# Attention in pairs of chunks: fp32 projections on quarters of the TensorE array, sums and numerators on halves

## The chip, the cores and the metric

The kernel runs on one core of a Trainium2 chip. The metric is the device time of one execution in microseconds. Three runs of the kernel before gave 926.39 us as their median (924.83 to 926.86).

## What is computed

A linear attention with random features (4 batches, 8 heads, 576 tokens, head size 64, 128 features), whose output of 2304 x 512 goes through two feed-forward blocks. All of it is in float32.

```python
def phi(x):
    proj = np.einsum('bhsd,md->bhsm', x, omega)
    sq = np.sum(x * x, axis=-1, keepdims=True) / 2.0
    h = proj - sq
    h = h - np.max(h, axis=-1, keepdims=True)
    return np.exp(h) / np.sqrt(m)
q_p, k_p = (phi(q_s), phi(k_s))
kv = np.einsum('bhsm,bhsd->bhmd', k_p, v)
z = np.sum(k_p, axis=2)
num = np.einsum('bhsm,bhmd->bhsd', q_p, kv)
den = np.einsum('bhsm,bhm->bhs', q_p, z)[..., None] + 1e-06
...
x = (x @ w_in) * sigmoid(x @ w_in) @ w_out
g = x @ w_gate
out = (g * sigmoid(g) * (x @ w_val)) @ w_out2
```

The term `sq` is the same for all features of a token, so it drops out against the row's maximum; the kernel leaves it out in both versions.

## The kernel before

**Stages.** The attention runs first (about the first 146 us), then the first feed-forward block (its upward products at L1066, its downward products at L1433), then the second one (the same lines). In the feed-forward blocks each fp32 product is made of three fp32r products of split operands, in seven products of Strassen's kind. The change touches the attention and the few instructions in which it hands over to the first upward phase.

**The attention's tiling.** The 32 pairs of batch and head are taken as 8 units `u`. A unit holds two heads (`h`) side by side on the 128 partitions of q and k, and two batches one after the other (`b`), so it has 1152 tokens, which are 9 chunks of 128 tokens. The fifth chunk of a unit holds the end of one batch and the beginning of the next one (64 tokens each). `step(s)` works on chunk s of 72; nothing is reordered, every engine runs its instructions in the order in which `step` writes them.

**One step.** `proj(s + 1)` makes the projections of q and k of the next chunk: six fp32r matmuls of 256 columns, three for each of q and k (high part times high part, low times high, high times low), where the 256 columns are the features of both heads, with zeros off the diagonal of omega. `soft(s)` takes the maxima of the four groups of 128 features on DVE (one reduction, `nb`) and then four exponentials on ACT (`kq`). `kv_tr(s - 2)` adds k' times v (and k' times ones) into a PSUM bank, two fp32 matmuls of 65 columns (four in the straddling chunk), and turns q' with two transposes; every second chunk ACT copies the turned q' of two chunks from PSUM to SBUF (`qp`, L816). When a batch has ended, DVE copies its sums out (`st`, L826) and the numerators follow two or more steps later: `num(u, g)` for three chunks (fp32 matmuls of 65 columns, 12 records in a plain group of three chunks, since an fp32 matmul is two records), `divide` on DVE, `turn` (three transposes), `take_out` on DVE, and one `store` for a unit.

**Splits.** q and k arrive as three pieces of 384 tokens per unit. `split_piece` makes the high and the low part of each piece on POOL (L706 and L708), for the first two pieces of the first unit partly on DVE.

**Banks.** PSUM has 8 banks. Projections and turned q' take banks 0 to 4 in rotation (`rot`), sums and numerators share banks 5 to 7 (`px`).

**Filling.** While the attention runs, `feed` puts in work for the stage after it, at most one instruction per engine and step for the stream "conv" (weights that are converted from 64-bit words and split: L343 and L408 on ACT, L350, L357, L406 and L419 on DVE, L376 on POOL) and a few for the stream "x" (the first block's input: L571 on ACT, L580 on DVE, L601). A consumer of an ACT or DVE result may go in one step later than its producer.

**Hand-over.** After the last step the last numerators of the last unit (two groups) are made inside the upward phase (`last_nums`, `last_turn`): `mark` writes a bank once (L1043) as soon as its divide has read it, so that the products can take it.

Of the kernel before, what the change touches and what calls it, by code (L numbers as in the profile page):

```python
# [9 lines left out]
F32 = mybir.dt.float32  # L10
# [32 lines left out]
def kernel(  # L43
# [21 lines left out]
    UB = 2  # L65
# [600 lines left out]
    rot = [0, 1, 2, 3, 4]  # L666
    px = deque((5, 6, 7))

    def bank():
        rot.append(rot.pop(0))  # L670
        return ps[rot[-1]].rearrange("p (a b) -> p a b", a=2)
# [10 lines left out]
    raw, hl, kq, qp, kvps = {}, {}, {}, {}, {}  # L682
# [14 lines left out]
    def load_piece(u, nm, i):  # L697
        raw[u, nm, i] = t = ap1.tile([P, CW], F32, tag=f"raw{nm}", name=f"raw{nm}", bufs=3)
        nc.sync.dma_start(out=t, in_=(kT if nm == "k" else qT)[u, :, i * CW : (i + 1) * CW])
# [15 lines left out]
    om = cut(fa, SUM_AT, 2 * M)  # L715
    zero = const.tile([P, M], F32, name="zero")
    nc.vector.memset(zero, 0.0)
    load_piece(0, "k", 0)
    for h in range(2):
        nc.sync.dma_start(out=om[h * D : (h + 1) * D, h * M : (h + 1) * M], in_=omT)  # L720
    load_piece(0, "q", 0)
    load_v(0, nc.scalar)
    for h in range(2):
        nc.vector.memset(om[h * D : (h + 1) * D, (1 - h) * M : (2 - h) * M], 0.0)
# [6 lines left out]
    for i in range(1, 3):  # L731
        for nm in ("k", "q"):
            load_piece(0, nm, i)
# [9 lines left out]
    PIECES = {3: (1, 0), 4: (1, 1), 6: (1, 2), 7: (1, 3), 0: (0, 4), 1: (0, 5)}  # L743
    pieces = [(nm, i) for i in range(3) for nm in ("k", "q")]


    act_q, dve_q, pps = [], [], {}
# [12 lines left out]
    def soft(s):  # L760
        ps = pps.pop(s)


        nb = ap1.tile([P, 4], F32, tag="nb", name="nb", bufs=3)
        nc.vector.reduce_max(nb, ps.rearrange("p i (h m) -> p (i h) m", h=2), axis=AX.X, negate=True)  # L765
        e = ap1.tile([P, 2, 2 * M], F32, tag="kq", name="kq", bufs=4)
        for i in range(2):
            for h in range(2):
                nc.scalar.activation(  # L769
                    e[:, i, h * M : (h + 1) * M],  # L770
                    ps[:, i, h * M : (h + 1) * M],
                    AF.Exp,
                    bias=nb[:, 2 * i + h : 2 * i + h + 1],
                )
        kq[s] = e
# [866 lines left out]
```

## Time and profile before

| | |
|---|---|
| runs, median | 926.39 us (924.83 to 926.86) |
| profiled execution, its own time | 926.11 us |
| span in the profile | 924.3 us |
| first product of the first upward phase (L1066) | 146.09 us after the span's start |
| PE busy, whole span | 905.0 us (98%) |
| DVE, ACT, POOL busy, whole span | 657.7, 558.4, 197.0 us |

The span is the time from the first to the last instruction; the execution's own time is 1.8 us longer. Busy time of PE counts matmuls in flight, which overlap, so that a busy PE is not PE at its peak. In the trace an fp32 matmul stands as two records, an fp32r matmul and a transpose as one.

### The profile page before, as it was taken

What the parts mean: (1) busy time and instruction counts of PE and PEld (TensorE: products, weight loads), DVE (VectorE), ACT (ScalarE), POOL (GpSimd) and SP (SyncE); (2) the same over time, 40 slices, a digit from 0 to 9 for tenths busy, and PEclk for the clock granted to TensorE, in tenths of its full rate; (3) what the DMA queues carried; (4) which work ended last, traced back from release to release, by engine and by line L of the source; (5) the groups of instructions that cost most, each with busy time, mean ns of one, the idle gap of its engine ahead of it and who ended that gap; (6) DMA issues with size and microseconds to landing.
All of it is one profiled execution on the core that took longest, in us unless ns stands there. A gap on an engine that the chain in (4) does not pass through costs nothing.

```text
span 924.3 us, 15768 instructions
## 1 busy us (share of the span) xinstructions
PE 905.0 (98%) x5591; PEld 895.3 (97%) x5591; DVE 657.7 (71%) x1055; ACT 558.4 (60%) x1190; POOL 197.0 (21%) x244
## 2 busy tenths in 40 slices
PE   8999999999999998999999999999999999999998
PEld 8999999999999998999999899999999999899998
DVE  4898986857574398586689899574747447968584
ACT  5788785876667675455457765554455447445453
POOL 6676951104343100000000014221303010000000
PEclk9999999999999999999999999999999999999999
DMA  7576515848989991715613755562626159371701
GB/s 218 183 235 208 174 50 197 271 157 275 317 291 358 349 382 58 232 55 163 206 43 109 244 164 187 174 201 79 213 68 222 47 184 314 114 240 52 237 16 69
DMA packets 109888, 169.94 MB, mean 184 GB/s; under 512 B 9200, under 2 KB 93808, under 8 KB 109808
## 3 DMA queue, kind: packets, MB, share of 16 engines
q1 hardware_dynamic: 108640, 168.33, 55.8%
q8 instruction: 44, 0.72, 0.3%
q10 hardware_dynamic: 1168, 0.59, 0.2%
q14 instruction: 36, 0.29, 0.1%
HBM read 107.02 MB, written 61.87 MB: 183 GB/s over the span
## 4 chain that ended last, share of the span: by engine, by line
PE 90%; DVE 4%; DMA 3%; ACT 2%; issue 1%; SPq 0%; DVEq 0%; ACTq 0%
PE ps L1066 43%; PE ps L1433 31%; PE ps L843 3%; PE ps L789 3%; PE ps L755 2%; PE ps L756 2%; PE ps L757 2%; PE ps L805 2%; DMA g_d<-fa 1%; PE ps L868 1%; DVE ra L1296 1%; DMA fa<-in_moe_w_in 1%; DVE ra L419 0%; DMA ra<-wu_val 0%; DVE fa L1124 0%
## 5 line engine op out<-in xcount | busy, mean ns | idle before, releaser
L376 POOL TENSOR_TENSOR fa<-fa 128x256 f32<-128x256 f32 x136 | 112.6, 841 | 529.0 <-DVE fa L357 301.3
L1066 PE MATMUL ps<-ra 128*128 128x384 f32 x840 | 156.3, 335 | 3.0 <-ACT ps L1083 3.0
L1066 PE MATMUL ps<-rb,ra 128*128 128x384 f32 x840 | 157.3, 340 | 0.0
L1066 PE MATMUL ps<-rc,ra 128*128 128x384 f32 x840 | 156.8, 339 | 0.0
L1066 PEld LDWEIGHTS ps<-ra 128*128 128x128 f32 x840 | 146.7, 188 | 4.3 <-ACT ps L1083 4.3
L1066 PEld LDWEIGHTS ps<-rb,ra 128*128 128x128 f32 x840 | 148.7, 188 | 0.3 <-ACT ps L1083 0.3
L1066 PEld LDWEIGHTS ps<-rc,ra 128*128 128x128 f32 x840 | 148.6, 188 | 0.1
L1083 ACT ACTIVATE ps<-ps 128x384 f32<-128x384 f32 x180 | 85.5, 476 | 88.7 <-PE ps L1066 82.1
L1140 DVE TENSOR_TENSOR fa<-fa,ps 128x384 f32<-128x384 f32 x120 | 66.2, 552 | 100.5 <-ACT ps L1083 78.1
L1292 ACT ACTIVATE ra<-fa 128x768 fp32r<-128x768 f32 x105 | 88.0, 844 | 81.2 <-PE ps L1433 64.4
L1296 DVE TENSOR_TENSOR ra<-fa,ra 128x768 fp32r<-128x768 f32 x105 | 100.5, 957 | 50.5 <-PE ps L1433 31.9
L1433 PE MATMUL ps<-ra,rb 128*128 128x384 f32 x720 | 129.4, 340 | 0.0
L1433 PEld LDWEIGHTS ps<-ra,rb 128*128 128x128 f32 x720 | 127.8, 189 | 0.8 <-DVE ra L1296 0.6
L1433 PE MATMUL ps<-ra 128*128 128x384 f32 x612 | 109.7, 337 | 6.7 <-DVE ra L1296 6.5
L1433 PEld LDWEIGHTS ps<-ra 128*128 128x128 f32 x612 | 106.7, 189 | 8.8 <-DVE ra L1296 8.0
L769 ACT ACTIVATE kq<-ps,nb 128x128 f32<-128x128 f32 x288 | 83.1, 403 | 25.3 <-DVE nb L765 24.1
L1433 PE MATMUL ps<-ra,rc 128*128 128x384 f32 x432 | 78.2, 340 | 1.6 <-DVE ra L1296 1.6
L1433 PEld LDWEIGHTS ps<-ra,rc 128*128 128x128 f32 x432 | 76.1, 188 | 2.7 <-DVE ra L1296 2.7
L1107 ACT ACTIVATE fa<-fa 128x384 f32<-128x384 f32 x84 | 43.8, 522 | 28.8 <-DVE fa L1140 28.5
L1316 DVE TENSOR_TENSOR fa<-ra,fa 128x768 f32<-128x768 f32 x63 | 60.1, 954 | 0.7
L1292 ACT ACTIVATE ra<-ra 128x768 fp32r<-128x768 f32 x42 | 35.5, 845 | 36.0 <-PE ps L1433 32.1
L1296 DVE TENSOR_TENSOR ra<-ra 128x768 fp32r<-128x768 f32 x42 | 40.2, 958 | 20.9 <-PE ps L1433 9.3
(100 smaller groups left out, 1227.6 us busy)
## 6 DMA issues: line engine op xcount, KB each, us to landing
g_d<-fa SPq DMA_DIRECT2D x168, 192.0 KB, 3.4
fa<-g_d SPq DMA_DIRECT2D x42, 384.0 KB, 4.4
ra<-g_d SPq DMA_DIRECT2D x42, 384.0 KB, 4.1
fa<-in_moe_w_out SPq DMA_DIRECT2D x28, 512.0 KB, 5.3
fa<-in_moe_w_in SPq DMA_DIRECT2D x16, 512.0 KB, 5.0
wd_out<-fa SPq DMA_DIRECT2D x14, 512.0 KB, 3.3
fa<-in_moe_w_gate SPq DMA_DIRECT2D x12, 512.0 KB, 3.9
fa<-in_moe_w_val SPq DMA_DIRECT2D x12, 512.0 KB, 5.2
```

The costliest lines, as they stand in the source:

```text
L376: f(blk(f"S{n}"), blk(l), blk(r))
L769: nc.scalar.activation(e[:, i, h * M : (h + 1) * M], ps[:, i, h * M : (h + 1) * M], AF.Exp, bias=nb[:, 2 * i + h : 2 * i + h + 1],)
L789: nc.tensor.matmul(acc[:, o : o + VH], e[a:z, 0, h * M : (h + 1) * M], v_t[u % 2][a:z, c, o : o + VH], start=first and h == 0, stop=last, ...
L843: nc.tensor.matmul(acc[a:z, o : o + VH], qp[u][:, h, c * P + a : c * P + z], st[u, b][:, h * VH : (h + 1) * VH], start=True, stop=True, sk ...
L1066: nc.tensor.matmul(ps[b][:, :N], cut(l, j * P, P), cut(r, j * N, N), start=start and c == 0, stop=stop and c == 5, skip_group_check=True,)
L1083: nc.scalar.activation(out() if callable(out) else out, src, AF.Copy)
L1107: nc.scalar.activation(b["t"], src, AF.Silu)
L1140: nc.vector.tensor_add(t, t if in_place else p5[n], ps[bank_][:, :N])
L1292: nc.scalar.activation(ops[s, p, k][0], src(), AF.Copy)
L1296: nc.vector.tensor_sub(l, src(), h.bitcast(F32))
L1316: (nc.gpsimd if eng == "POOL" else nc.vector).tensor_sub(z(PLACE[to]), z(PLACE.get(l, l)), z(PLACE.get(r, r)))
L1433: nc.tensor.matmul(ps[BANKS[p] + e][:, :N], cut(a, e * P, P), b, start=p in FIRST and i == 0 and c == 0, stop=p in LAST and i == fp - 1 an ...
```

## The change

`two_steps(d)` takes the place of `step(s)` and works on a pair of chunks; 36 pairs make the attention.

- `proj(d)` uses fp32 matmuls on q and k as they arrived. Each has 64 rows of the array (one head) and 64 columns of it (half a chunk's tokens), so that four of them stand on the four quarters of the array; omega has 128 columns for each. A pair of chunks takes 16 of them. The two heads write into different banks; a pair takes two banks, and pairs alternate between banks 0, 1 and 2, 3.
- The splits of q and k (`split_piece`) and of omega are gone, and so is POOL's share of this stage but for `feed`. q and k of a unit arrive as one transfer each, except for the first unit.
- `soft(d)` has one reduction and four exponentials for each bank, as many of both as before. Divides stand between the two reductions.
- `kv` and `num` are written as halves: each matmul yields 64 of the 128 output partitions.
- `q_turn(d)` turns q' of both chunks into bank 4, and one copy on ACT takes the 512 columns out.
- `feed` is called twice for a pair, at its end. Three groups of numerators are left for the upward phase where there were two.

```diff
-    rot = [0, 1, 2, 3, 4]
     px = deque((5, 6, 7))
...
-    def split_piece(u, nm, i):
-        hi, lo = hl[u, nm, i] = tuple(
-            ap1.tile([P, CW], F32R, tag=f"{x}{nm}", name=f"{x}{nm}", bufs=3) for x in ("hi", "lo")
-        )
-        t = raw.pop((u, nm, i))
-        nc.gpsimd.tensor_scalar(hi, t, 1.0, 1.0, op0=ALU.mult, op1=ALU.mult)
-        eng = nc.vector if u == 0 and i < 2 else nc.gpsimd
-        eng.tensor_sub(lo, t, hi.bitcast(F32))
-        if u + 1 < NU and u > 0:
-            load_piece(u + 1, nm, i)
+    def load_raw(u, nm, i=None):
+        if not i:
+            raw[u, nm] = ap1.tile([P, UT], F32, tag=f"raw{nm}", name=f"raw{nm}", bufs=2)
+        src = kT if nm == "k" else qT
+        a, z = (0, UT) if i is None else (i * CW, (i + 1) * CW)
+        nc.sync.dma_start(out=raw[u, nm][:, a:z], in_=src[u, :, a:z])
...
-    om_hi = const.tile([P, 2 * M], F32R, name="om_hi")
-    om_lo = const.tile([P, 2 * M], F32R, name="om_lo")
-    nc.vector.tensor_scalar_mul(om_hi, om, SCALE)
-    nc.vector.scalar_tensor_tensor(om_lo, om, SCALE, om_hi.bitcast(F32), op0=ALU.mult, op1=ALU.subtract)
...
+    nc.vector.tensor_scalar_mul(om, om, SCALE)
...
-    def proj(s):
-        u, c = divmod(s, NCH)
-        ps = bank()
-        for i, nm in enumerate(("k", "q")):
-            hi, lo = hl[u, nm, c // 3]
-            cs = slice((c % 3) * P, (c % 3 + 1) * P)
-            nc.tensor.matmul(ps[:, i, :], hi[:, cs], om_hi, start=True, stop=False)
-            nc.tensor.matmul(ps[:, i, :], lo[:, cs], om_hi, start=False, stop=False)
-            nc.tensor.matmul(ps[:, i, :], hi[:, cs], om_lo, start=False, stop=True)
-        pps[s] = ps
...
+    def proj(d):
+        for j in range(2):
+            u, c = divmod(2 * d + j, NCH)
+            for i, nm in enumerate(("k", "q")):
+                o = (2 * j + i) * M
+                for t in HALF:
+                    for h in range(2):
+                        r = slice(h * D, (h + 1) * D)
+                        nc.tensor.matmul(
+                            ps[2 * (d % 2) + h][t : t + D, o : o + M],
+                            raw[u, nm][r, c * P + t : c * P + t + D],
+                            om[r, :],
+                            start=True,
+                            stop=True,
+                            skip_group_check=True,
+                        )
+
+    def soft(d, between):
+        e = kq[d] = ap1.tile([P, 2, 2, 2 * M], F32, tag="kq", name="kq", bufs=3)
+        for h in range(2):
+            x = ps[2 * (d % 2) + h].rearrange("p (g m) -> p g m", g=4)
+            nb = ap1.tile([P, 4], F32, tag="nb", name="nb", bufs=4)
+            nc.vector.reduce_max(nb, x, axis=AX.X, negate=True)
+            for g in range(4):
                 nc.scalar.activation(
+                    e[:, g // 2, g % 2, h * M : (h + 1) * M], x[:, g, :], AF.Exp, bias=nb[:, g : g + 1]
                 )
...
+    def kv(d, parts):
+        e, ended = kq[d], []
+        for u, b, c, j, a, z in parts:
+            first = (u, b) not in kvps
             if first:
                 kvps[u, b] = px.popleft()
+            LEFT[u, b] -= 1
             for h in range(2):
                 o = h * VH
+            if not LEFT[u, b]:
+                ended.append((u, b))
+        return ended
+
+    def q_turn(d):
+        e, t = kq.pop(d), ps[4].rearrange("p (h s) -> p h s", h=2)
+        for j in range(2):
+            for h in range(2):
+                nc.tensor.transpose(t[:, h, j * P : (j + 1) * P], e[:, j, 1, h * M : (h + 1) * M], ident)
+        qp[d] = ap1.tile([P, 2, 2 * P], F32, tag="qp", name="qp", bufs=9)
+        act_q.append(lambda: nc.scalar.activation(qp[d], t, AF.Copy))
...
+            d, j = divmod(u * NCH + c, 2)
+            for h in range(2):
+                o = (c - g * GC) * VW + h * VH
+                for b, a, z, _, _ in runs(c * P, (c + 1) * P):
+                    for t in HALF:
+                        if a <= t < z:
+                            nc.tensor.matmul(
+                                acc[t : t + D, o : o + VH],
+                                qp[d][:, h, j * P + t : j * P + t + D],
+                                st[u, b][:, h * VH : (h + 1) * VH],
+                                start=True,
+                                stop=True,
+                                skip_group_check=True,
+                            )
...
+    def two_steps(d):
+        step_of[0] = 2 * d
+        if d + 1 < ND:
+            proj(d + 1)
...
+        for f in act_q:
+            f()
         act_q.clear()
+        if 0 <= d < ND:
+            soft(d, between)
+        else:
+            for f in between:
+                f()
+        taking("DVE")
+        ended, whole = [], []
+        if 1 <= d <= ND:
+            whole, split = kv_parts(d - 1)
+            ended += kv(d - 1, split)
+            ended += kv(d - 1, whole)
...
+            u, g, _ = groups.pop(0)
+            num(u, g)
+            to_divide.append((u, g))
+        if 1 <= d <= ND:
+            q_turn(d - 1)
+        for x in turns:
+            turn(*x)
+            to_take.append(x)
+        to_turn.extend(to_divide)
+        for u, b in ended:
+            kv_evac(u, b)
+            groups.extend((u, g, d) for g in ((1, 2) if b else (0,)))
...
+        if d < ND:
+            done_kv, done_proj = 2 * d, 2 * d + 4
+            for u in range(1, NU):
+                if u not in v_in and done_kv > (u - 1) * NCH:
+                    v_in.add(u)
+                    load_v(u)
+                for i, nm in enumerate(("k", "q")):
+                    if (u, nm) not in raw and done_proj > (u - 1) * NCH + 2 * i + (0 if u == 1 else 2):
+                        load_raw(u, nm)
+            for s in (2 * d, 2 * d + 1):
+                step_of[0] = s
+                if s >= 8:
+                    feed("conv", s, {"SP": 1, "ACT": 1, "DVE": 1, "POOL": 1})
+                if s >= 27:
+                    feed("x", s, {"SP": 4, "ACT": 2, "DVE": 2, "POOL": 1})
+
...
+        for (u, g, _), b in zip(left_over, (7, 6, 5)):
+            num(u, g, b)
+        for u, g, _ in left_over:
+            divide(u, g)
```

PE, in the middle of the attention: before, one step with the numerators behind it. Names are out<-in; `ps_84` is the bank of the sums, `ps_85` that of the numerators, `ps_80` the one of the turned q', `ps_82` the next one of the projections.

```order
L789 MATMUL ps_84<-v_98,kq 128x65 x2
L805 MATMUL ps_80<-ident,kq 128x128 x2
L843 MATMUL ps_85<-st,qp 128x65 x2
L843 MATMUL ps_85<-st,qp 64x65 x4
L843 MATMUL ps_85<-st,qp 128x65 x2
L755 MATMUL ps_82<-om_hi,hik 128x256
L756 MATMUL ps_82<-om_hi,lok 128x256
L757 MATMUL ps_82<-om_lo,hik 128x256
```

PE at the same place of the change: the end of one pair's projections, then sums, numerators, both chunks' turned q', one group's turn and the next projections.

```order
L738 MATMUL ps_78<-om,rawq 64x128
L738 MATMUL ps_79<-om,rawq 64x128
L782 MATMUL ps_85<-v_98,kq 64x65 x8
L829 MATMUL ps_84<-st,qp 64x65 x12
L798 MATMUL ps_82<-ident,kq 128x128 x4
L854 MATMUL ps_83<-ident,nt 128x128 x3
L738 MATMUL ps_80<-om,rawk 64x128
L738 MATMUL ps_81<-om,rawk 64x128
```

Sums and numerators stand as matmuls with 64 output partitions behind each other, and between them and the projections stand transposes on the whole array.

DVE with an "x" feed, before: the two subtractions L580, whose high parts ACT makes in L571, stand one reduction behind the step in which ACT got them.

```order
L765 TENSOR_REDUCE nb<-ps_78 128x4
L877 COPY fa<-ps_83 128x384
L357 SCALAR_TENSOR_TENSOR fa<-fa 128x512
L580 TENSOR_TENSOR ra<-fa,ra 128x384
L580 TENSOR_TENSOR ra<-xr_89,ra 128x384
L765 TENSOR_REDUCE nb<-ps_79 128x4
```

DVE at the same place of the change (L752 is the reduction, L809 the copy of the sums).

```order
L752 TENSOR_REDUCE nb<-ps_79 128x4
L809 COPY st<-ps_84 128x130
L350 TENSOR_SCALAR fa<-fa 128x512
L357 SCALAR_TENSOR_TENSOR fa<-fa 128x512
L580 TENSOR_TENSOR ra<-fa,ra 128x384
L580 TENSOR_TENSOR ra<-xr_89,ra 128x384
L752 TENSOR_REDUCE nb<-ps_80 128x4
L752 TENSOR_REDUCE nb<-ps_81 128x4
```

The copy of the sums and two steps' feed now stand together ahead of the next pair's first reduction.

## Rows read from the trace of the kernel before

**Rows 1.** Busy time by stretch: PE, PEld, DVE, ACT, POOL, granted clock, DMA share, GB/s.

```profile
20.00:140.00 120.00, 120.00 (x1113) 117.63 (x1111) 103.70 (x205) 97.68 (x316) 84.20 (x100) 1.00 0.54 170
```

**Rows 2.** The chain that ended last, 20 to 54 us: start, length, what.

```profile
23.85 0.39 PE ps L789 x4
24.24 0.22 PE ps L805 x2
...
25.18 0.39 PE ps L789 x4
...
25.79 0.33 PE ps L868 x3
...
33.90 0.60 PE ps L789 x8
...
38.87 1.29 PE ps L843 x12
...
46.18 1.37 PE ps L843 x16
...
51.31 0.60 PE ps L789 x8
```

**Rows 3.** Instructions in order of time, PE, narrow windows around 64 us.

```profile
63.93 0.34 PE L843 MATMUL ps<-st,qp 128*64 128x65 f32 x4
...
64.10 0.29 PE L843 MATMUL ps<-st,qp 128*64 128x65 f32 x4
...
64.16 0.49 PE L843 MATMUL ps<-st,qp 128*64 128x65 f32 x3
...
64.17 0.47 PE L843 MATMUL ps<-st,qp 128*64 128x65 f32 x2
```

**Rows 4.** The same view, 138.3 to 139.2 us.

```profile
138.35 0.67 PE L789 MATMUL ps<-v,kq 64*128 64x65 f32 x8
138.94 0.44 PE L805 MATMUL ps<-ident,kq 128*128 128x128 f32 x2
```

**Rows 5.** The same view, all engines, the first 24 us.

```profile
1.05 3.06 PEld L735 LDWEIGHTS ps<-zero 128*128 128x128 f32 x14 [1.05 <-DVE zero L717]
...
6.53 0.63 POOL L706 TENSOR_SCALAR hiq<-rawq 128x384 fp32r<-128x384 f32 x1 [2.79 <-DMA rawq<-in_q]
```

**Rows 6.** The same view, ACT, 67 to 74 us.

```profile
68.72 0.54 ACT L571 ACTIVATE ra<-xr 128x384 fp32r<-128x384 f32 x1
69.14 0.61 ACT L816 ACTIVATE qp<-ps 128x512 f32<-128x512 f32 x1
69.61 1.17 ACT L769 ACTIVATE kq<-ps,nb 128x128 f32<-128x128 f32 x4
70.62 0.73 ACT L343 ACTIVATE fa<-fa 128x512 f32<-128x512 f32 x1
71.94 1.14 ACT L769 ACTIVATE kq<-ps,nb 128x128 f32<-128x128 f32 x4 [0.59 <-DVE nb L765]
```

**Rows 7.** The same view, DVE, 69 to 76 us.

```profile
71.17 0.68 DVE L765 TENSOR_REDUCE nb<-ps 128x4 f32<-128x512 f32 x1
71.77 0.28 DVE L826 COPY st<-ps 128x130 f32<-128x130 f32 x1
71.97 1.01 DVE L350 TENSOR_SCALAR fa<-fa 128x512 uint32<-128x512 uint32 x1
...
73.51 0.15 DVE L855 TENSOR_SCALAR rc<-ps 128x6 f32<-128x6 f32 x1
...
74.39 0.68 DVE L357 SCALAR_TENSOR_TENSOR fa<-fa 128x512 uint32<-128x512 uint32 x1
```

**Rows 8.** Groups by line and shape, DVE, 20 to 140 us and 160 to 240 us: count, busy us, mean ns.

```profile
L580 DVE TENSOR_TENSOR ra<-xr,ra 128x384 fp32r<-128x384 f32 x7 | 6.6, 943 | 0.3 <-ACT ra L571 0.3
...
L580 DVE TENSOR_TENSOR rb<-xr,rb 128x384 fp32r<-128x384 f32 x6 | 3.3, 549 | 0.2 <-ACT rb L571 0.2
```

**Rows 9.** Instructions in order of time, PE, 143 to 152.5 us.

```profile
146.09 1.20 PE L1066 MATMUL ps<-ra 128*128 128x384 f32 x6
...
151.08 0.45 PE L1043 MATMUL ps<-ra 128*128 128x384 f32 x1 [0.85 <-DVE nt L858]
```

**Rows 10.** Busy time by stretch, around 354 us (columns as in the first group).

```profile
352.00:354.00 2.00, 0.00 (x0) 0.00 (x0) 2.00 (x4) 0.36 (x1) 0.00 (x0) 0.97 0.00 0
354.00:358.00 4.00, 3.90 (x14) 3.90 (x15) 2.84 (x5) 0.42 (x1) 0.00 (x0) 0.59 0.00 0
```

More of the change, by code (lines that the diff above doesn't have):

```diff
@@ L760, in soft @@
[L760 to L768, printed above, removed]
+    nc.vector.tensor_scalar_mul(om, om, SCALE)
+    act_q, dve_q, ND = [], [], NSTEP // 2
+    def proj(d):
[14 more added lines that the diff above has]
+                        )
@@ L772, in soft @@
-                    AF.Exp,
-                    bias=nb[:, 2 * i + h : 2 * i + h + 1],
-                )
-        kq[s] = e
-    tps = {}
-    def kv_tr(s):
-        u, c = divmod(s, NCH)
-        e = kq[s]
-        ended = []
-        for b, a, z, first, last in runs(c * P, (c + 1) * P):
+                    e[:, g // 2, g % 2, h * M : (h + 1) * M], x[:, g, :], AF.Exp, bias=nb[:, g : g + 1]
+                )
+            if h == 0:
+                for f in between:
+                    f()
@@ L785, in kv_tr @@
                 kvps[u, b] = px.popleft()
-            acc = ps[kvps[u, b]]
+            LEFT[u, b] -= 1
             for h in range(2):
                 o = h * VH
-                nc.tensor.matmul(
-                    acc[:, o : o + VH],
-                    e[a:z, 0, h * M : (h + 1) * M],
-                    v_t[u % 2][a:z, c, o : o + VH],
-                    start=first and h == 0,
-                    stop=last,
-                    skip_group_check=True,
-                )
-            if last:
-                ended.append(b)
@@ L817, in kv_tr @@
-        return [(u, b) for b in ended]
+                for t in HALF:
+                    nc.tensor.matmul(
+                        ps[kvps[u, b]][t : t + D, o : o + VH],
+                        e[a:z, j, 0, h * M + t : h * M + t + D],
+                        v_t[u % 2][a:z, c, o : o + VH],
+                        start=first and h == 0,
+                        stop=not LEFT[u, b],
+                        skip_group_check=True,
+                    )
+            if not LEFT[u, b]:
+                ended.append((u, b))
@@ L953, with taking @@
-    for s in range(NSTEP + LAG):
-        step(s)
+    def two_steps(d):
+        step_of[0] = 2 * d
+        if d + 1 < ND:
+            proj(d + 1)
+        divides, turns, takes = to_divide[:], to_turn[:], to_take[:]
+        for x in (to_divide, to_turn, to_take):
+            x.clear()
+        between = [lambda x=x: divide(*x) for x in divides]
+        def taking(eng):
+            for x in takes:
+                take_out(*x, eng)
+                if x[1] == GC - 1:
+                    stores.append((d + 1, x[0]))
+        for f in act_q:
+            f()
+        act_q.clear()
+        if 0 <= d < ND:
+            soft(d, between)
+        else:
+            for f in between:
+                f()
+        taking("DVE")
[4 more added lines that the diff above has]
+            ended += kv(d - 1, whole)
+        coming = sum((u, b) not in kvps and LEFT[u, b] == NCH // 2 + 1 for u, b in {x[:2] for y in kv_parts(d) for x in y}) if 0 <= d < ND else 0
+        if groups and groups[0][2] < d and len(px) and len(px) - 1 + len(turns) + len(ended) >= coming and not (groups[0][:2] != (NU - 1, 0) and groups[0][0] == NU - 1) and d < ND:
+            u, g, _ = groups.pop(0)
[10 more added lines that the diff above has]
+            groups.extend((u, g, d) for g in ((1, 2) if b else (0,)))
+        for x in stores[:]:
+            if x[0] <= d:
+                stores.remove(x)
+                store(x[1])
+        if d < ND:
[13 more added lines that the diff above has]
+                    feed("x", s, {"SP": 4, "ACT": 2, "DVE": 2, "POOL": 1})
@@ L955 @@
+    stores, v_in = [], {0}
+    for d in range(-1, ND + 1):
+        two_steps(d)
     for name in ("conv", "x"):
@@ L978, in end_attention @@
     def end_attention():
-        step(NSTEP + LAG)
-    waits = [True]
+        two_steps(ND + 1)
+        two_steps(ND + 2)
+        left_over.extend(groups)
+        assert not (to_divide or to_turn or to_take or stores) and all(u == NU - 1 for u, _, _ in groups)
+    waits, left_over = [True], []
     def last_space():
```

137 lines of the change are left out of this document (25 added, 112 removed).

## The prediction

> **What bounds the kernel now.** I read the busy time by stretch first. From 20 to 140 us PE is busy for all 120 us, DVE for 103.70, ACT for 97.68, POOL for 84.20, with the full clock granted [rows 1]. Then the chain that ended last: in this stage it holds nothing but PE, and it has a period. The straddling chunk's sums start at 33.90 and again at 51.31 us [rows 2], so a unit takes 17.41 us, and a pair of chunks (4.5 to a unit) 3.87 us. The 120 us therefore hold 31 pairs, and the other engines spend on a pair 103.70 / 31 = 3.35 us (DVE) and 97.68 / 31 = 3.15 us (ACT). The reader is to see that PE sets the pace, but that DVE and ACT stand only 0.5 and 0.7 us a pair behind it. The first product of the next stage starts at 146.09 us [rows 9]; from there on the program is the same but for a few instructions, and I carry any shift of that mark unchanged to the end. The sum is made against the profiled execution's 926.1 us, 0.3 us under the median of the three runs.
>
> **PE's work, before.** One step from 23.85 to 25.18 is 1.33 us, of which 0.39 are sums and 0.22 the two transposes, so 0.72 are the projections [rows 2], 1.44 for a pair. A plain group of numerators (12 records) is 1.29, which is 0.108 a record.
>
> **Halves.** The straddling group shows them already. Its 16 records take 1.37 [rows 2]; 8 of them are whole ones at 0.108, so its 8 halves take 0.51 with the way into the form and out of it. Inside, the halves run two at a time: the third pair starts at 64.10, the fourth at 64.16 and 64.17 [rows 3], so 0.06 buys two records, where one whole record costs 0.108. Four pairs are 0.24, and the other 0.27 are two changes of form, 0.13 each. For a unit:
> - sums: 8 whole chunks x 4 pairs x 0.06 = 1.92, plus the straddling chunk, 16 records on quarters, four at a time, 0.24: 2.16 (before 8 x 0.39 + 0.60 = 3.72);
> - numerators: 72 records, 36 pairs, 2.16 (before 2 x 1.29 + 1.37 = 3.95);
> - q' transposes as before, 18 x 0.11 = 1.98, and the groups' transposes 3 x 0.33 = 0.99 [rows 2];
> - changes of form: projections to sums, numerators to transposes, transposes to projections, 3 for each pair, 13.5 x 0.13 = 1.76.
>
> **Quarters.** No row shows an fp32 record with 64 columns of array and 128 moving columns, nor four at a time. Above: the warm-up's fp32 records, 128 columns on the whole array, stand 3.06 / 14 = 0.219 apart [rows 5] in a stretch where all matmuls run at half the later pace, so 0.109 at full pace. Below: 0.06, as the halves have it with 65 columns. The duration should follow the columns that move, twice as many as in the halves, so I take 0.109. Of concurrency the rows show two column halves [rows 3] and also two row halves: eight records of 64 rows in the 0.59 us from 138.35 to 138.94 [rows 4], both ends' changes of form in it, where eight whole ones would take 0.86. Two by two makes four, so a pair's 32 records take 8 x 0.109 = 0.87, and a unit 3.92.
>
> The Trainium skill, "TensorE: Matmul & The Clock Gate", Part 3, reports a measured 3.07 times for four tiles on rows, short of four. By that the projections of a pair would take 32 x 0.109 / 3.07 = 1.14, an estimate, and the sum below would give about 910. No run here shows four tiles at once.
>
> PE's sum for a unit: 2.16 + 2.16 + 1.98 + 0.99 + 1.76 + 3.92 = 12.97, which is 2.88 a pair. With the lower bound of a quarter (0.06) it is 2.49, and with quarters two at a time (1.74 a pair) 3.76.
>
> **The other engines, which now count.** Reductions and exponentials keep number and size. DVE gets nothing new; it loses POOL as a neighbour. L580 took 943 ns beside POOL's splits and 549 later [rows 8]: seven times 0.39 is 2.8 us, and I count as much again for its other instructions of that kind, 5.5 in all, 0.18 a pair. The lower bound of this gain is nothing. So DVE goes to 3.17 and ACT stays at 3.15; both include tails that the next instruction overlaps: a reduction lasts 0.68 but the next starts after 0.60 [rows 7], and ACT's copy of q' lasts 0.61 but the next starts after 0.47 [rows 6]. No engine can do a pair in less than 2.9. That the splits leave POOL is worth nothing by itself, since no PE wait on them shows in the chain after the start. One transfer per unit in place of three is issued 2.5 to 3.5 pairs ahead, 8 us or more, and costs nothing as long as it lands in that time.
>
> **Waits that the new order brings.** (a) A pair's projections need the banks of the pair two before it, so PE starts pair d's turn when ACT has ended the exponentials of d - 1, about 0.2 later. (b) ACT's copy of q' stands ahead of the next exponentials and needs the transposes, which stand behind projections, sums and numerators: 0.2 + 0.87 + 0.13 + 0.48 + 0.72 + 0.13 + 0.44 + 0.2 = 3.2 after that start. ACT has by then done a copy and eight exponentials, 0.47 + 8 x 0.25 = 2.5 [rows 6], and waits up to 0.7 less what is fed. (c) DVE's copy of the sums needs the sums, 0.2 + 0.87 + 0.13 + 0.48 + 0.3 = 2.0 after the start; behind it stand two steps' feed (about 1.1 with two L580), then the next reduction, 0.77 from its start to the exponentials (71.17 to 71.94 [rows 6, 7]): 3.9, where ACT would be free at 2.5 + 0.5 + its feed. (d) Where ACT makes a high part and DVE subtracts it in the same pair, DVE waits out ACT's exponentials. These overlap with one another and fall on some pairs only. I take 3.25 us a pair: DVE's 3.17 and 0.08 of such waits. The bounds are 2.9 (no wait, tails overlapped) and 3.6 (0.4 a pair).
>
> **Start and end.** The last input of the first projections lands at 6.53, where POOL could begin with it [rows 5]. From 6.6: 8 x 0.219 = 1.75 at the slow pace, 0.77 and a little latency, 2.0 of exponentials: PE begins the second turn at 11.5. Then 35 turns, and 1.7 for the last sums and transposes: 11.5 + 35 x 3.25 + 1.7 = 127.0 instead of 146.1, so -19.1. The hand-over: before, PE takes the second mark at 151.08, 5.0 after the first product [rows 9]. Three groups left over are 3 x 0.72 of numerators and three divides of 0.88 (73.51 to 74.39 [rows 7]) on DVE, 1.0 + 0.8 + 2.7 + 0.2 = 4.7, and one more turn is 0.33: nothing. So 926.1 - 19.1 = **907.0 us**.
>
> **Rivals.**
> - *PE's gain is cut more by the ring of waits* (b to d), 3.55 a pair: 11.5 + 124.3 + 1.7 = 137.5, so 917.5. For it: DVE and ACT are within 10% of the new pace, each in strict order, with two sets of banks instead of five in rotation.
> - *Quarters are quicker and waits fall into gaps*, 2.9 a pair: 114.7, so 894.7. For it: halves take 0.06; against it: DVE's 3.17.
> - *Quarters run two at a time* (slower). Then PE needs 3.76 a pair, and the wait for the banks adds about 0.2: 3.96, 151.8, so 931.8. For it: no row has four tiles at once. Against it: rows and columns each show two streams at once. It decides from 3.80 a pair on, where the mark is at 146.1 again; projections above 1.6 us a pair reach that.
> - *The clock falls.* After 2 us without a matmul the granted clock was 0.59 of full on average in 354 to 358 us [rows 10], a mix of the levels 2.4 and 1.2 GHz. PE will idle in each turn, but under 1 us at a time. If seven turns ran at 1.2 GHz, each 2.5 longer: +17, 924.
> - *Copying, not TensorE, sets the pace.* The Trainium skill, "TensorEngine Tiling (Array Packing)", PSUM Bottleneck, warns that tiling speeds up the matmuls but not the emptying of PSUM. By it the quarters' exact price does not matter below 2.9; the rows agree, as DVE's 3.17 is above PE's 2.88, and that is the case forecast.
>
> **How the numbers follow.** Forecast (3.05 to 3.45 a pair, 900 to 914): 0.55. Ring of waits (to 3.75): 0.18. Quicker: 0.12. Two at a time: 0.10. Clock: 0.05. No change to be measured is within 0.2% (1.9 us) of before; I give it 0.03, out of the ring's far end and the clock. Slower by more: the two-at-a-time case and a little of the clock, 0.11. Faster: 0.86. From 895 to 924 leaves out most of the two-at-a-time case, some of the clock's, and the quick case's far end, about 2 in 10.
>
> **What would show it.** Right: the first L1060 (today's L1066) near 127 us; pairs of about 3.2 us; four quarter records within 0.03 us of each other and the next four 0.11 later; PE idle for some tenths in each turn, released by ACT's exponentials; DVE busy above 90% in the stage; L580 near 0.55. Wrong: quarter records standing in twos, 0.06 or more between them; a granted clock of 0.5 in the stage; ACT waiting for transposes or DVE by more than 0.5 a pair.

## The result

The changed kernel takes 916.95 us (median of four runs, 914.45 to 919.76), the kernel before, run beside it, 925.95 (924.83 to 926.86): a ratio of 0.990, 95% interval [0.987, 0.993]. That is 9.0 us less, where 19.1 were forecast: the change is faster, the range of 895 to 924 holds the time, and the forecast of 907.0 was 10 us too low.

The first product of the next stage, which answers to [rows 9], and the hand-over behind it (PE in order of time; start, length, what, and in brackets the idle time ahead of it and what ended it):

```profile
136.99 1.23 PE L1060 MATMUL ps<-ra 128*128 128x384 f32 x6
138.15 2.32 PE L829 MATMUL ps<-st,qp 128*64 128x65 f32 x72
141.94 0.62 PE L1037 MATMUL ps<-ra 128*128 128x384 f32 x2 [1.46 <-DVE nt L844]
```

So the mark moved by 136.99 - 146.09 = -9.1, where -19.1 was forecast, and the hand-over still takes 5.0: the median's whole miss of 10 us is already there at the end of the attention. The stage by busy time (columns of [rows 1]), and DVE's groups that answer to [rows 8]:

```profile
20.00:133.00 113.00, 101.23 (x2226) 85.07 (x2227) 94.95 (x205) 97.16 (x311) 20.48 (x24) 0.97 0.56 187
```

```profile
L580 DVE TENSOR_TENSOR ra<-xr,ra 128x384 fp32r<-128x384 f32 x7 | 4.6, 662 | 0.0
L580 DVE TENSOR_TENSOR ra<-fa,ra 128x384 fp32r<-128x384 f32 x7 | 4.3, 612 | 6.0 <-ACT ra L571 6.0
```

No engine is busy throughout any more, DVE least of the three (84%), and L580 waits 6.0 us for ACT, 0.3 before [rows 8]. The exponentials of the 36 pairs begin at 9.07 (the first) and 133.04 us (the last): 3.54 us a pair. But there are two kinds of pair. Those of pairs 10 and 31 begin at 39.5 and 121.9: 21 pairs, between which most of the next stage's work is fed, at 3.92 us. The other 14 take 2.97.

The chain that ended last, from 40 to 122 us, by engine, tile and line (the answer ends where the line does), and a piece of it in order of time:

```profile
by line: ACT kq L754 22.2%; DVE nb L752 20.6%; issue 7.9%; DVE ra L419 6.5%; DVE nt L844 5.5%; DVE ra L580 4.1%; PE ps L798 3.8%; PE ps L829 3.5%; DVE fa L357 3.3%; PE ps L738 3.2%; ACT ra L571 2.6%; DVE xt L863 2.4%; DVE rc L842 2.2%; ACT 
...
70.86 1.15 ACT kq L754 x4
72.01 0.42 ACT ra L571
72.43 0.02 issue
72.45 0.04 DVE ra L580
72.48 0.44 issue
72.92 0.55 DVE ra L580
73.47 0.60 DVE nb L752
74.08 0.08 DVE rc L841
...
74.41 0.56 DVE nt L844
74.96 0.60 DVE nb L752
75.56 0.47 DVE fa L863
76.03 0.04 issue
76.08 0.92 PE ps L829 x24
```

Before, this view held PE alone [rows 2]. Now DVE has 50% of it, ACT 28% and PE 14%, and up to 76.08 us this piece is a ring without PE: the last exponentials of a pair, behind them on ACT the high part that was fed (L571), for which DVE waits with the low part (L580), and behind that on DVE the next pair's reduction, the divide and the second reduction, for which ACT waits. From 70.86 to the end of the next pair's second reduction (74.96 and its 0.60) is 4.7 us.

The same stretch on PE, where eight records of quarters stand 0.22 apart:

```profile
72.20 0.45 PE L738 MATMUL ps<-om,rawk 64*64 64x128 f32 x8
72.47 0.40 PE L738 MATMUL ps<-om,rawq 64*64 64x128 f32 x8
72.69 0.40 PE L738 MATMUL ps<-om,rawk 64*64 64x128 f32 x8
72.91 0.40 PE L738 MATMUL ps<-om,rawq 64*64 64x128 f32 x8
73.24 0.69 PE L782 MATMUL ps<-v,kq 128*64 128x65 f32 x16
76.08 0.34 PE L829 MATMUL ps<-st,qp 128*64 128x65 f32 x4 [2.15 <-DVE fa L863]
```

### The profile page after: what moved, and what is told of

Its sections match the earlier page's. It is cut to its first block, busy times and chain, and to the rows that moved or that the text cites. A ratio compares the mean times of both kernels' runs of the same rounds, so it can differ in the third digit from the quotient of the medians.

```text
span 917.6 us, 18106 instructions
## 1 busy us (share of the span) xinstructions
PE 883.3 (96%) x6887; PEld 856.2 (93%) x6887; DVE 641.3 (70%) x1048; ACT 558.0 (61%) x1186; POOL 120.8 (13%) x152
## 4 chain that ended last, share of the span: by engine, by line
PE 73%; DVE 12%; ACT 7%; DMA 5%; issue 2%; POOL 0%; SPq 0%; ACTq 0%; DVEq 0%; POOLq 0%
PE ps L1060 38%; PE ps L1427 31%; ACT kq L754 3%; DVE nb L752 2%; DMA fa<-in_moe_w_out 2%; PE ps L738 1%; DVE ra L419 1%; DVE ra L1290 1%; PE ps L798 1%; DVE fa L357 1%; DVE nt L844 1%; PE ps L782 1%; DMA rb<-wd_out 1%; DVE fa L1134 1%; DMA wd_out<-fa 1%
## 5 line engine op out<-in xcount | busy, mean ns | idle before, releaser
L376 POOL TENSOR_TENSOR fa<-fa 128x256 f32<-128x256 f32 x136 | 111.8, 836 | 604.6 <-DVE fa L357 368.9
L754 ACT ACTIVATE kq<-ps,nb 128x128 f32<-128x128 f32 x288 | 80.0, 398 | 15.8 <-DVE nb L752 12.2
L1101 ACT ACTIVATE fa<-fa 128x384 f32<-128x384 f32 x84 | 43.8, 522 | 29.5 <-DVE fa L1134 29.2
L1290 DVE TENSOR_TENSOR ra<-ra 128x768 fp32r<-128x768 f32 x42 | 40.2, 958 | 20.9 <-PE ps L1427 9.3
```

Source lines behind the costliest of these rows:

```text
L376: f(blk(f"S{n}"), blk(l), blk(r))
L754: nc.scalar.activation(e[:, g // 2, g % 2, h * M : (h + 1) * M], x[:, g, :], AF.Exp, bias=nb[:, g : g + 1])
L1101: nc.scalar.activation(b["t"], src, AF.Silu)
L1290: nc.vector.tensor_sub(l, src(), h.bitcast(F32))
```

## The experiments

Edits are against the changed kernel. "Last pair" is the start of the last pair's exponentials, "mark" the first product of the next stage, both in us from the start of the profiled execution's span; "pairs 4 to 35" is the time from the exponentials of pair 4, behind which the feed begins, to those of the last pair, 35 (pairs are counted from 0); time and ratio are of all runs.

| kernel | last pair | pairs 4 to 35 | mark | median us | ratio to before, 95% |
|---|---|---|---|---|---|
| changed kernel | 133.0 | 112.0 | 137.0 | 916.95 | 0.987 to 0.993 |
| no_feed | 112.2 | 93.1 | 145.4 | 940.19 | 1.013 to 1.017 |
| feed_gap | 125.9 | 104.8 | 129.8 | 909.12 | 0.980 to 0.985 |
| num_last | 132.7 | 113.5 | 136.6 | 917.40 | 0.989 to 0.993 |
| div_after | 130.6 | 110.5 | 134.6 | 915.23 | 0.986 to 0.989 |
| gap_num_last | 127.0 | 107.0 | 130.9 | 911.40 | 0.982 to 0.986 |
| gap_num_div | 123.9 | 104.8 | 127.8 | 907.86 | 0.979 to 0.982 |
| gap_xdve | 120.4 | 101.2 | 124.7 | 908.08 | 0.979 to 0.982 |
| pair_guard | 123.7 | 104.4 | 127.6 | 908.17 | 0.979 to 0.983 |
| whole_no_feed | 137.0 | 113.7 | 171.0 | 967.83 (one run) | - |
| whole | 141.9 | 118.6 | 146.2 | 927.22 | 0.999 to 1.004 |
| before_gap | - | - | 148.1 | 926.98 | 1.000 to 1.003 |
| best | 122.5 | 103.4 | 126.8 | 908.64 | 0.979 to 0.984 |
| guard_xdve | 124.9 | 105.8 | 129.2 | 909.98 | 0.982 to 0.985 |
| gap_xdve_one | 121.3 | 101.1 | 125.2 | 911.97 | 0.985 to 0.988 |

The column without the first pairs is needed because the profiled executions differ there by 1.8 us, although nothing is fed ahead of pair 4. In the changed kernel pair 2 begins 4.83 us behind pair 1, in no_feed 3.04; the sums of that turn took 1.14 us, where they take 0.69 later on. In div_after they took the same 1.14, and there the granted clock is on record: 0.50, the lower of its two levels, 1.2 GHz (PE in the changed kernel, and busy time by stretch in div_after):

```profile
13.21 1.14 PE L782 MATMUL ps<-v,kq 128*64 128x65 f32 x16
```

```profile
11.30:14.20 2.90, 2.90 (x42) 2.38 (x34) 1.29 (x2) 1.16 (x5) 0.00 (x0) 0.50 0.75 229
```

Pair 2 came as late in feed_gap, gap_num_last and gap_xdve_one. In whole and whole_no_feed the clock was low until 21.6 and 21.4 us. In the other runs the second turn ran at full pace. Why they differ stays open.

**no_feed**: nothing fed between the pairs.

```diff
-                if s >= 8:
-                    feed("conv", s, {"SP": 1, "ACT": 1, "DVE": 1, "POOL": 1})
-                if s >= 27:
-                    feed("x", s, {"SP": 4, "ACT": 2, "DVE": 2, "POOL": 1})
```

> Nothing of the next stage's preparation (weights L343 to L419, first X operands L571 and L580) is issued between the pairs; all of it comes after the attention. Theory A (in the changed kernel the prepared work, which falls on pairs 11 to 31 alone, sets their 3.7 us through DVE's and ACT's strict order): every pair takes about 3.0 us, as pairs 4 to 10 do, so the last pair's exponentials start at 113 to 117 us of the span instead of 133.0. Rival B (the banks and the numerators' waits set the pace whatever is fed): 3.4 us a pair or more, last pair at 128 or later. The total is no verdict: the same work is then done where nothing covers it, which should cost 10 us or more at the hand-over.

Theory A held, and the last pair came a little earlier than its bound: (112.24 - 9.01) / 35 = 2.95 us a pair. The chain from 40 to 100 us is PE's alone:

```profile
by line: PE ps L738 36.4%; PE ps L782 22.3%; PE ps L798 19.2%; PE ps L829 15.2%; PE ps L854 7.1%
```

The new order of the attention by itself runs at PE's pace, close to the 2.88 of the prediction's sum. The rest is the feed's doing. Where nothing covers that work, the last pair and the mark lie 33.1 us apart instead of 4.0, so it has to stand between the pairs all the same.

**feed_gap and pair_guard**: the same work is fed, but nothing made in the same pair is used. feed_gap does it by a gap of two steps, pair_guard by the pair:

```diff
-made[k] = (s, {"SP": 5 if name == "x" else 3, "POOL": 2}.get(e, 1))
+made[k] = (s, {"SP": 5 if name == "x" else 3, "POOL": 2}.get(e, 2))
...
-if any(k in made and s - made[k][0] < made[k][1] for k in o.ins):
+if any(k in made and (s - made[k][0] < made[k][1] or s // 2 == made[k][0] // 2) for k in o.ins):
```

> A fed instruction may use what another engine made only from the next pair on, not from the same pair. Theory A1 (DVE's waits for a high part that ACT makes in the same pair, 10.5 us in the changed kernel's trace, pass on to the reductions and so to the exponentials): those waits fall below 2 us and the last pair's exponentials start 7 to 10 us earlier (123 to 126 instead of 133.0); total 908 to 911 if the hand-over doesn't give it back. Rival A2 (DVE has that time to spare, since the reductions wait for projections anyway): the waits go and the last pair starts within 2 us of 133.0; total 915 to 919.

> The guard in its exact form: what was made in a pair may be used from the next pair's first step on (feed_gap also forbids that where it was made in a pair's second step). Theory A1 (waits inside a pair are the whole cost): the last pair's exponentials start at 125 to 128 us as in feed_gap and the remaining feed after the loop is shorter, mark at 128 to 130, total 907 to 910. Rival A3 (what helped in feed_gap is that less was fed per pair, not that waits went): the last pair comes at 129 or later, and total 911 to 915.

In the changed kernel DVE waited in this way 10.5 us (who waited for whom, 20 to 133 us: total, times, longest):

```profile
DVE ra L580 <- ACT ra L571: 6.0, 7, 1.4
...
DVE fa L350 <- ACT fa L343: 2.7, 2, 1.4
...
DVE ra L419 <- ACT ra L408: 1.8, 2, 1.1
```

In feed_gap and pair_guard none of these rows is left. In feed_gap the last pair comes 7.2 us earlier, in pair_guard 9.3, of which 1.8 are the first pairs': from pair 4 on it is 7.2 and 7.6. The totals are 7.8 and 8.8 us lower. Ahead of the last pair all three kernels run the same fed work, 28 instructions on ACT, 48 on DVE and 24 on POOL, so it is the waits that went, and not work. A1 held (its bound for pair_guard's last pair missed by the first pairs' 1.8), A2 and A3 fell. The 21 fed pairs now take 3.53 (feed_gap, 39.2 to 113.3).

**num_last** and **div_after**:

```diff
...
-            u, g, _ = groups.pop(0)
-            num(u, g)
-            to_divide.append((u, g))
         if 1 <= d <= ND:
             q_turn(d - 1)
         for x in turns:
             turn(*x)
             to_take.append(x)
...
+            u, g, _ = groups.pop(0)
+            num(u, g)
+            to_divide.append((u, g))
```

```diff
-            if h == 0:
-                for f in between:
-                    f()
+        for f in between:
+            f()
```

> TensorE's order in a pair becomes projections, sums, transposes of q', turn, numerators, instead of numerators ahead of the transposes. Theory C (the numerators' wait for one of the three banks, 6.4 us of idle TensorE with a granted clock of 0.5 for 3.4 us after each of the two longest, holds up the transposes, ACT's copy of q' and so the exponentials): the two gaps of over 2 us and the two dips of the clock at 77 and 111 us are gone, the mark comes 5 to 9 us earlier (128 to 132 instead of 137.0), total 908 to 912. Rival B2 (the wait moves with the numerators, and the next projections stand behind them): mark within 1.5 us of 137.0, total 915 to 919.

> A divide (0.9 us on DVE) stands behind both reductions of a pair, not between them. Theory D (the second reduction is late by the divide and the exponentials wait for it; the trace has 3.3 us of that in four places, and 6.0 us of other waits for reductions): last pair's exponentials 3 to 6 us earlier than 133.0, total 911 to 914. Rival C (what is late is the bank that a divide, turn and take_out give back): the divide comes later by 0.7 us where DVE is behind, numerators wait longer, and the mark moves by less than 1.5 us or comes later; total 915 to 920.

num_last: B2 held. The numerators wait 2.5 us in all (0.5 at most) for `take_out`, but the next sums 4.5 (three times, 2.1 at most), so the wait moved with its bank. One of the two dips of the clock is gone (1.00 from 60 to 100 us), and still nothing is gained (113.5 us from pair 4 on, 112.0 in the changed kernel), with pairs of the same length: the pairs that begin at 66.7, 74.2 and 109.0 us in the changed kernel come 5.04, 4.74 and 5.28 us behind the ones ahead of them, here 5.04, 4.73 and 5.28. So PE's wait for a bank does not set the pace while the ring of ACT and DVE is there. div_after: 1.6 us off the pairs ((130.6 - 8.2) against (133.0 - 9.1)), near rival C's bound and below theory D's; the total is inside the changed kernel's runs, so this one is unclear.

**gap_num_last and gap_num_div**: feed_gap with num_last, and with both.

> The guard of feed_gap (nothing made in the same pair is used) and numerators behind the transposes and the turn. In feed_gap four waits of sums or numerators for a bank that take_out frees are left, 3.9 us of idle TensorE with one dip of the granted clock (0.91 in 100 to 120 us). Theory C2 (that wait counts only now, when the feed's waits no longer cover it): these four waits fall to under 1.5 us, last pair's exponentials at 121 to 124 us instead of 125.9, total 905 to 908. Rival C3 (in num_last the place of the numerators moved no pair; DVE's take_out comes when it comes): last pair within 1 us of 125.9, total 908 to 911.

> As gap_num_last, and the divide behind both reductions. If exponentials that wait for the second reduction matter (1.1 us in two places for L841 and 1.5 us in six for reductions in feed_gap), 1 to 3 us less than gap_num_last. If the bank's return matters more, the same or up to 3 us more, since the divide, the turn and take_out come later.

C2 fell, and C3 held but for its bounds: last pair 127.0, 911.40; from pair 4 on it is even some 2 us longer than feed_gap. With the divide behind as well it is 123.9 and 907.86, 3.5 us less, and the pairs from 4 on are as long as feed_gap's. Against feed_gap the total is 1.3 us less with intervals that overlap: unclear.

**gap_xdve, best, guard_xdve and gap_xdve_one**: the X operands' differences (L601) on DVE, with feed_gap's guard; with pair_guard's and both edits of order; with pair_guard's alone; and with feed_gap's and at most one fed X instruction for each step on ACT and DVE.

```diff
-    early["x"].extend(x_prep(0, 0, xr1, False, "POOL", early=True))
+    early["x"].extend(x_prep(0, 0, xr1, False, "DVE", early=True))
...
-                    feed("x", s, {"SP": 4, "ACT": 2, "DVE": 2, "POOL": 1})
+                    feed("x", s, {"SP": 4, "ACT": 1, "DVE": 1, "POOL": 1})
```

> The guard of feed_gap, and the eight differences of the first X operands (L601) on DVE instead of POOL. In feed_gap L580 takes 1.36 us beside POOL's L601 and 0.55 otherwise, and L601 takes 1.0 to 1.3 on POOL. Theory E (POOL as a neighbour costs DVE in the pairs 26 to 31): DVE gains up to 4 x 0.8 = 3.2 and pays 8 x 0.56 = 4.5 for the differences: last pair's exponentials 1 to 3 us later than 125.9, no L580 above 0.7 us, total 909 to 912. Rival F (the chain load, difference, high part, low part gets shorter by a pair each time, so that less is left after the loop): the mark comes 1 to 3 us earlier than 129.8 although the last pair comes later.

gap_xdve did better than either theory said: the last pair comes 5.5 us earlier than in feed_gap, 3.6 of them from pair 4 on, with more work on DVE. 3.18 us a pair is the quickest of the fed kernels, the granted clock is 1.00 from 20 to 120 us, and PE leads the chain again:

```profile
by line: PE ps L738 19.2%; PE ps L782 12.6%; PE ps L798 10.3%; DVE nb L752 10.1%; ACT kq L754 9.3%; PE ps L829 6.4%; DVE ra L580 5.3%; issue 4.1%; DVE nt L844 3.4%; PE ps L854 3.3%; DVE xt L863 2.5%; ACT qp L800 2.2%; DVE ra L419 1.9%; ACT 
```

F's part (the mark 5.1 us earlier) was nearer. What of it is DVE's shorter instructions and what the shorter chain of load, difference and parts is not told apart. Nor is a third cause: ahead of the last pair stand three high parts, three low parts and two differences fewer than in feed_gap, which come behind it. Of the total only 1.0 us shows against feed_gap, within both intervals: what stands behind the mark gave the rest back (below).

> All that helped, together: the exact guard of pair_guard, the differences of gap_xdve on DVE, numerators behind the transposes and the divide behind both reductions as in gap_num_div. If the gains add up in part, 3.05 to 3.2 us a pair, the last pair at 116 to 120.5 us, mark at 120 to 124, and, with 2 to 4 us lost behind the mark as in gap_xdve, a total of 903 to 907. If DVE's work now sets the pace (3.15 to 3.2 a pair), no better than gap_xdve: 907 to 909.

> The exact guard and the eight differences on DVE, in the changed kernel's order. Theory J (the order with the divide behind and the numerators last costs here, since with DVE's work at 3.15 us a pair each late divide, turn and take_out is waited for): last pair's exponentials at 118 to 121 us against 122.5 in best, mark at 122 to 125, total 905 to 908. Rival K (the exact guard feeds more into each pair, and that is what best lost against gap_xdve): last pair at 122 to 124, total 908 to 910.

The gains did not add up. guard_xdve came 2.4 us later than best (124.9 against 122.5), where J had it earlier, so J fell and K stands, its bound missed by 0.9: the exact guard lets four fed instructions stand on DVE ahead of a reduction, three of them at twice their 0.55 us beside POOL's L376, and ACT waits 2.6 us (in order of time):

```profile
98.77 0.55 DVE L580 TENSOR_TENSOR ra<-xr,ra 128x384 fp32r<-128x384 f32 x1
...
98.93 2.99 POOL L376 TENSOR_TENSOR fa<-fa 128x256 f32<-128x256 f32 x3 [2.64 <-DVE fa L357]
...
99.24 1.09 DVE L580 TENSOR_TENSOR ra<-fa,ra 128x384 fp32r<-128x384 f32 x1
...
100.25 1.08 DVE L580 TENSOR_TENSOR ra<-xr,ra 128x384 fp32r<-128x384 f32 x1
...
101.26 1.08 DVE L601 TENSOR_TENSOR fa<-fa 128x384 f32<-128x384 f32 x1
102.26 0.68 DVE L752 TENSOR_REDUCE nb<-ps 128x4 f32<-128x512 f32 x1
...
102.86 0.15 DVE L841 TENSOR_SCALAR rc<-ps 128x6 f32<-128x6 f32 x1
103.03 1.14 ACT L754 ACTIVATE kq<-ps,nb 128x128 f32<-128x128 f32 x4 [2.58 <-DVE rc L841]
```

> gap_xdve with at most one fed instruction of the X operands for each step on ACT and DVE instead of two. Theory L (bunches of fed work between two reductions are what is left): no pair from 26 to 31 above 3.8 us (in gap_xdve 4.59 and 3.96), last pair at 117 to 120 instead of 120.4, total 905 to 908. Rival M (the work itself counts, wherever it stands, or less is fed and the rest is done uncovered after the loop): last pair at 119.5 to 121 and the mark at 124.5 or later, total 908 to 911.

L fell: no pair from 26 to 31 is above 3.9 us, and from pair 4 on the attention still takes 101.1 us, 101.2 in gap_xdve. M is nearer, though its total (908 to 911) is missed: the last pair comes at 121.3, and what was not fed is done behind the mark: the mark is 20.9 us earlier than before, the sixtieth product behind it only 16.4.

**whole and whole_no_feed**: sums and numerators on the whole array again, projections on quarters, with and without feed.

```diff
...
-                        ps[kvps[u, b]][t : t + D, o : o + VH],
-                        e[a:z, j, 0, h * M + t : h * M + t + D],
+                        ps[kvps[u, b]][:, o : o + VH],
+                        e[a:z, j, 0, h * M : (h + 1) * M],
...
-                                acc[t : t + D, o : o + VH],
-                                qp[d][:, h, j * P + t : j * P + t + D],
+                                acc[a:z, o : o + VH],
+                                qp[d][:, h, j * P + a : j * P + z],
```

> no_feed, where TensorE is busy for 92.0 of 92 us and a pair takes 2.95 us, with sums and numerators on the whole array again (projections stay on quarters). By the prices of the prediction a pair's sums go from 0.52 to 8 x 0.108 = 0.86, a group of numerators from 0.80 to 1.29 in two pairs of three, and the change of form ahead of the transposes (0.13) goes: 0.34 + 0.33 - 0.13 = 0.54, so 3.4 to 3.6 us a pair and the last pair's exponentials at 128 to 135 us instead of 112.2. Rival G (halves gain little, the weight loads set the pace either way): under 3.15 a pair, last pair before 120. The total is no verdict.

> The changed kernel with sums and numerators on the whole array, feed as it was. If TensorE's time were on the path in every pair, 35 x 0.54 = 19 us more: last pair at 150 instead of 133.0, total 933 to 937. Theory A (in the fed pairs, 11 to 31, the feed's waits set the pace, and TensorE idles for some half a microsecond a pair): the extra lands in idle time there and only pairs 1 to 10 and 32 to 35 pay in full, 5 to 12 us: last pair at 138 to 145, total 921 to 928.

Without feed the halves are worth (113.71 - 93.07) / 31 = 0.67 us a pair from pair 4 on, more than the 0.54 priced; G fell. With feed the last pair comes 8.9 us later than in the changed kernel, and from pair 4 on it is 6.6 us instead of 20.6: some two thirds of what the halves save on PE fall into waits, as theory A has it. And `whole`, which is pairs, quarters and no splits without the halves, is as fast as the kernel before.

**before_gap**: feed_gap's edit in the kernel before.

> The kernel before, with feed_gap's guard alone. Theory A (the same-pair waits cost only because TensorE no longer is the pace): TensorE is busy throughout in the kernel before, so the first product stays within 0.7 us of 146.1 and the total within 2 us of before. Rival H (the guard would help any order): first product 3 to 8 us earlier, total below 922.

The total is 1.1 us more, with an interval from 1.000 to 1.003, as theory A had it. The mark of the profiled execution is 2.0 later, which neither theory had; why stays open. H fell: while PE was the pace these waits cost nothing, and there were few (0.3 us for L580, 1.8 for L350).

## Why the prediction was wrong

**The step that failed** is "I take 3.25 us a pair: DVE's 3.17 and 0.08 of such waits". The waits (c) and (d) were named, with their mechanism, and then priced as if they overlapped with one another and with DVE's work. In the fed pairs they follow one another in a ring: the term was 0.08 x 35 = 2.8 us, and DVE alone waited for ACT's fed parts eleven times, 10.5 us in all. Its length could have been added up from the rows of before: half the exponentials 1.0, one high part 0.4, two low parts 1.1 (twice [rows 8]'s 0.55), two reductions 1.2 and a divide 0.9 [rows 6, 7] make 4.6 us, against 4.7 measured. With 0.08 of waits the fed pairs' DVE work, 69.81 / 21 = 3.32, would have given 3.40 us for 21 pairs; with the other 14 at their measured 2.97 that is 3.23 a pair, next to the forecast. Measured are 3.92: 0.52 x 21 = 10.9 us, where the mark misses by 10.0. Of these 10.0 the slow second turn has 1.8, which stand in the 14 pairs' 2.97; without them the mark would have missed by 8.2.

**Why the wait is new.** `feed` lets a consumer go one step behind its producer. Before, a step's reduction and exponentials lay between the two. In the new order the feeds of both steps of a pair stand together, so that "one step later" is the next instruction. Neither the prediction nor its rows looked at the guard from that side. feed_gap and pair_guard show this cause, which makes 7.2 and 7.6 us of the pairs from 4 on and 7.8 and 8.8 of the total; before_gap shows that the same guard is worth nothing in the kernel before.

**Prices on PE** (a pair of chunks whose numerators did not wait).

```profile
65.32 0.69 PE L782 MATMUL ps<-v,kq 128*64 128x65 f32 x16
65.84 0.87 PE L829 MATMUL ps<-st,qp 128*64 128x65 f32 x24
66.64 0.33 PE L798 MATMUL ps<-ident,kq 128*128 128x128 f32 x1
```

Quarters: 8 records in 0.22 us, 0.88 a pair and the change of form on top (72.20 to 73.24), where 0.87 and 0.13 were taken. The Trainium skill, "TensorE: Matmul & The Clock Gate", Part 3, has 3.07 times for four tiles on rows; by that 32 records would have taken 1.14, an estimate. The measured 0.88 is that of four at full rate, if a single quarter takes the 0.109 assumed; no run here shows one alone. From start to start the sums took 0.52 (0.48 forecast), numerators with the change of form behind them 0.80 (0.85). The sum of 2.88 a pair measured 2.95 where nothing is fed. The halves' worth was too small by 0.1 a pair.

**The other engines.** DVE was forecast above 90% busy with 3.17 a pair; it was 84%, with 94.95 / 113 x 3.54 = 2.97. An average over the stage hid that the fed pairs need 3.32 and the others less. L580 fell to 0.61 and 0.66 rather than 0.55: POOL kept its L376 and L601.

**Start, end and carry.** PE's second turn began at 11.29 (11.5 forecast), but it ran at half pace still, which the forecast gave to the first turn alone: the 1.8 us above. From the last exponentials' end (135.29) to the mark it was 1.7, as forecast. The hand-over, costed at nothing, was 5.0 as before.

**The rivals.** The ring of waits, given 0.18 with 3.55 a pair, a mark of 137.5 and 917.5 us, is what happened, to 0.6 us, and that it is so near is in part luck: its 3.55 had no slow second turn in it. Two at a time did not happen. "Copying, not TensorE, sets the pace" (the Trainium skill, "TensorEngine Tiling (Array Packing)", PSUM Bottleneck): PE did leave the lead of the chain, as the rule has it, but no_feed shows that reductions, exponentials and copies of a pair fit under PE's 2.95. What set the pace above that was the fed work and its place. **The clock**, at the lower level at the start, fell twice more in the attention, each time behind a gap in PE's work, here 2.15 us for `take_out` (busy time by stretch, columns as in [rows 1]):

```profile
74.00:76.10 2.10, 0.02 (x2) 0.02 (x2) 1.96 (x6) 1.65 (x6) 0.00 (x0) 1.00 0.86 223
...
77.30:80.70 3.40, 3.40 (x46) 2.74 (x46) 3.31 (x8) 2.53 (x9) 0.00 (x0) 0.52 1.06 384
```

0.52 is the lower level, but for the stretch's last tenth; so it was once more from 111.4 to 114.7 us, behind a gap of 2.48. "Under 1 us at a time" was wrong for three gaps (1.03, 2.15 and 2.48). What these two dips cost was not measured by itself; num_last has one of them and no quicker pairs.

**Behind the mark** the profiled execution (919.76 us, the longest of the four) lost part of its gain. At 176.36 ACT's L1101 has waited 2.87 us for a transfer out (g_d), PE stands still for 2.08, and the granted clock is 0.51 from 179.5 to 183.0; compared product by product with the kernel before, 10.3 us of lead become 6.6. Near 350 us 1.4 come back. Both kernels stand still there alike, the changed one for 2.30 us and the one before for 2.31 (PE, first the changed kernel, then the one before):

```profile
347.44 1.14 PE L1427 MATMUL ps<-ra 128*128 128x384 f32 x5 [2.30 <-DVE ra L1290]
```

```profile
354.10 1.97 PE L1433 MATMUL ps<-ra 128*128 128x384 f32 x5 [2.31 <-DVE ra L1296]
```

But behind it the granted clock is 1.00 in the changed kernel (347 to 351 us) and 0.59 in the one before [rows 10], so these 1.4 us are the clock's and not the change's doing. The median is 9.0 lower, as the mark's 9.1 carried to the end would have it; the marks of the other three executions are not on record. pair_guard lost 4.2 and gap_xdve 2.1 us at the late transfer. Why that transfer is late in some executions stays open. So does how the 0.2 to 0.3 us by which the pairs of gap_xdve and best lie above no_feed's divide between DVE's work and waits.

## What to carry to other kernels

When a change takes the bounding engine off the path, walk the ring that is left, instruction by instruction through one pair with all that is fed into it, instead of adding a small wait to the next busiest engine's average; and do it for each kind of pair. A distance counted in steps is worth what stands between two steps: when two are merged, every guard that counts them has to be looked at again. Work that fills an engine's gaps costs nothing only as long as another engine sets the pace.

## What the runs showed of the hardware

DVE's subtractions on 128 x 384 elements took 1.08 to 1.09 us instead of 0.55 while POOL ran even its small 128 x 256 differences (0.9 to 1.0 us each in guard_xdve). With eight of POOL's larger differences on DVE, 0.55 each, gap_xdve's pairs from 4 on took 3.6 us less than feed_gap's; that this is POOL's absence is not shown, since less fed work stood ahead of the last pair too.

The clock fell not in a gap but after it: 1.1 us after the matmuls had begun again at 76.08 us, and it stayed at half for 3.4 us of full work. The length of the gap alone does not say whether it falls. In the changed kernel it fell behind gaps of 2.15 and 2.48 us and not behind those of 1.46 (the hand-over above) and 2.30 (near 347 us); in feed_gap it fell behind one of 1.53 (108.92 to 110.45 us, then a granted clock of 0.50 from 111.0 to 114.4), and in best not behind one of 2.14 (101.44 to 103.59).
